# Chunked linear attention and a two-layer block: x of the first two chunks written in the order of q's columns, with a written-out order of operations

## Chip, cores and metric

The kernel runs on one core of a Trainium2 chip. The metric is the device time in microseconds (us) of one execution. The core has five engines with an instruction queue each: TensorE (PE), VectorE (DVE), ScalarE (ACT), GpSimd (POOL) and SyncE (SP). SP only issues DMAs here; ACT and POOL issue some too. Each engine works its queue strictly in order and waits on semaphores for the others.

## What is computed

q, k and v are float32 of shape (4, 8, 768, 64): batch, heads, tokens, head width. For each head, attention without softmax runs over blocks of 64 tokens with a decay lam:

```
intra = (q_b k_b^T * Dmask) v_b
inter = (q_b * lam_pow) kv_state
out_b = intra + inter
kv_state = lam^64 * kv_state + (k_b * rev_pow)^T v_b
```

The heads of a token, side by side, are x (3072 tokens by 512), and the rest is

```
h = x @ w_in                  # 512 -> 2048
g = h + sin(alpha*h)^2 / (alpha + 1e-9)
out = g @ w_out               # 2048 -> 512
```

## The kernel before

The 3072 tokens are worked on in six chunks of 512. The attention of a chunk is done by four *quads*; a quad is 256 tokens of four heads. Quads 0 to 3 (function quad0) make chunk 0, quads 4 to 7 chunk 1, and the sixteen behind them (function quad) make chunks 2 to 5 by another layout. In quad0, t = 4 ch + 2 u + jj: u is the half of the chunk's tokens, jj the half of the heads.

Every operation is recorded with a tag, and the documents name operations by these tags, with the quad or the chunk and block behind them:

- qs, ks, vs: scaling of q (L936) and k (L949) and the cast of v (L963, L966) to bf16
- Tq, Tk: transposes on TensorE (L977); cT: their copies to SBUF (L980)
- S: the product of q and k (L1020); mask: its masking on VectorE (L1025)
- Z: the product of k and v (L1037); Zi, Z with a digit, Zs: casts and sums of the state (L1056, L1110, L1122)
- I, O: what state and masked product give to the attention's output (L1067, L1082), in two PSUM banks
- x: the cast of these banks to xT in bf16 (L1099 for chunks 0 and 1, L1283 behind them)
- A: x @ w_in for one block of 128 of the 2048 columns (L1330); an ending h0 or h1 is a half of the chunk, and a final e the part of a product that is started early
- sin, sq, g: sine on ACT (L1342), its square on ACT (L1349), VectorE or POOL (L1350), and g on VectorE (L1354); g frees the PSUM bank of A
- B: g @ w_out (L1407); oh, o: its eviction (L1416, L1420, L1423); st: the store (L1426)
- w0 to w3 and w4 to w7: the loads of the blocks of w_in and w_out on POOL's queue (L793, L800, L805)
- quad k4.0 and the like: the loads of chunks 0 and 1 on SP's queue (L891, L897), load k4.0 and the like those of later chunks (L775, L784)

In chunks 0 and 1, q is loaded so that a partition holds four successive tokens. Its transposed columns therefore stand in the order (e, b): first the tokens 4b, then 4b+1, and so on, in groups of 32 within a block of 128. S, I and O carry this order on into the PSUM banks. piece_x puts the tokens back in order as it casts: it reads 32 elements in a row and writes every fourth element of xT:

```
o = xT[x][:, 2*jj:2*jj+2, 256*u:256*u+256].rearrange("p a (i b e) -> p i a e b", i=2, e=4)
i = M_ps[:, a:b + 1:b - a, :].rearrange("p i (a e b) -> p i a e b", e=4, b=32)[:, :, 0:2]
```

The order of the work is found at build time by a planner (Program.schedule). It plays through the program with a cost for each operation and takes, on each engine, the operation that can start first, with small hand-set shifts of rank (TURN), earliest times for the weight loads (HOLD) and an added lateness for loads (LATE). It hands out the six PSUM banks, fills long gaps of TensorE before 60 us with products of zeros (L754; one is counted at 0.4267 us until COLD, 0.2157 after it), and adds a wait of a POOL operation for the last VectorE operation that shares a port with it. GATE lets a load of chunk 1 wait for a named operation; a name that no operation bears is no wait, and q has no gate with a second digit of 1. In the plan a cast of x costs 0.585 us on ACT and 0.65 on VectorE. ENG0, ENG1, X0, X1, SQ0 and SQ1 say which engine does an operation; BOTH in X1 splits a cast in a half on ACT and one on VectorE.

From chunk 1's A on, TensorE alternates A of the next chunk with B of the current one, and one quad of a later chunk is worked in between.

Of the kernel before, what the change touches and what calls it, by code (L numbers as in the profile page):

```python
# [242 lines left out]
          'x7.1': -20},  # L243
    SQ0=('DVE', 'ACT', 'POOL', 'POOL', 'DVE', 'ACT', 'ACT', 'POOL', 'ACT', 'ACT', 'ACT', 'ACT', 'ACT', 'DVE', 'DVE',
         'POOL'),
# [11 lines left out]
    CUTS=(0, 256, 384, 512),  # L257
    GATE={'q4.0': 'Tk1', 'q6.0': 'Tk0', 'q6.1': 'A0.4', 'v4.0': 'O2'},
    SPLIT=(1, 1, 0, 1),
# [6 lines left out]
          {'c': ('ACT', 'DVE'), 'k': 'DVE', 'p': 2, 'q': 'DVE', 'v': 'ACT', 'w': 'DA', 'z': 'DD'},  # L266
          {'c': ('DVE', 'ACT'), 'k': ('DVE', 'POOL'), 'p': 2, 'q': 'DVE', 'v': 'ACT', 'w': 'AA', 'z': 'AD'},
          {'c': ('DVE', 'ACT'),
# [5 lines left out]
           'z': 'AA'}),  # L274
    X0=('ACT', 'DVE', 'DVE', 'DVE'),
    ENG1=({'c': 'ACT', 'k': ('POOL', 'DVE'), 'p': 0, 'q': 'DVE', 's': 0, 'v': 'POOL', 'w': 'DD', 'z': 'DD'},
          {'c': ('DVE', 'ACT'),
# [24 lines left out]
    LATE={'D': 0.5, 'l': 1, 'q': 0},  # L302
    COLD=10.5,
    FSL=0.05,
)

# [30 lines left out]
class Program:  # L337
# [9 lines left out]
    def __init__(self, nbanks, fill=None, fill_until=0.0, window=12, hold=None, turn=None):  # L347
        self.hold, self.turn = hold or {}, turn or {}
        self.ops = []
        self.writer = {}  # L350
        self.readers = {}
        self.slots = {}
        self.nbanks = nbanks
        self.fill = fill
        self.fill_until = fill_until
        self.window = window
        self.nb = 0
        self.late = {}

    def bank(self):  # L360
# [3 lines left out]
    def add(self, eng, fn, lat=0.0, occ=None, reads=(), writes=(), slot=None, work=0.0, weight=1.0, after=(),  # L364
# [3 lines left out]
        if port is None:  # L368
            port = "whole" if eng == "POOL" else ""
        self.ops.append(op)  # L370
# [37 lines left out]
    def schedule(self):  # L408
# [9 lines left out]
        left = {op: len(op.deps) + len(op.soft) for op in ops}  # L418
        ready = {op: self.hold.get(op.tag, 0.0) for op in ops}
        free = {e: 0.7 for e in self.ENGINES}  # L420
        pend = {e: [] for e in self.ENGINES}
# [8 lines left out]
        def held(e="SP"):  # L430
            return sum(q[0].desc * (q[1] / q[0].work if q[0].work else 1.0) for q in queues[e]) - self.RING
# [25 lines left out]
        while done < len(ops) or any(queues.values()):  # L457
            best = None
            for e in self.ENGINES:
                if e == "PE":  # L460
                    picks = []
                    for i, op in enumerate(pe[:60]):
# [16 lines left out]
                else:  # L479
                    if not pend[e] or (e == "SP" and held() > 0):  # L480
                        continue
                    can = pend[e] if e != "ACT" or held(e) <= 0 else [o for o in pend[e] if o.slot is None]
                    if not can:
                        continue
# [90 lines left out]
            order.append(op)  # L575
            done += 1
            for u in op.soft_users:
# [82 lines left out]
def bass_lightning_attn__then__act_snake_kernel(  # L660
# [12 lines left out]
    DM = H * D  # L673
# [23 lines left out]
    with es:  # L697
# [58 lines left out]

        P = Program(NPS, fill=zero_mms, fill_until=60.0, window=12, hold=HOLD, turn=TURN)
        P.narrow_until = TUNE["NARROW"]
        P.cold, P.slack = TUNE["COLD"], TUNE["FSL"]
        P.late = TUNE["LATE"]  # L760
        rec = P.add
# [108 lines left out]
        def alpha_ops():  # L870
            rec("ACT", lambda e: e.dma_start(alpha_r[:, :], moe_alpha.rearrange("(m p) -> m p", p=128)),
                writes=["alpha_r"], slot="alpha", work=0.1, weight=9.0, desc=16, tag="alpha")
            vb = P.bank()
# [28 lines left out]
        def quad0(ch, u, jj, engs, engs2):  # L902
# [187 lines left out]
            def piece_x(eng="ACT"):  # L1090
                def io(y):
                    o = xT[x][:, 2 * jj:2 * jj + 2, 256 * u:256 * u + 256].rearrange("p a (i b e) -> p i a e b", i=2, e=4)
                    a, b = banks[0].i, banks[1].i
                    i = M_ps[:, a:b + 1:b - a, :].rearrange("p i (a e b) -> p i a e b", e=4, b=32)[:, :, 0:2]
                    return (o, i) if y is None else (o[:, y], i[:, y])
# [298 lines left out]
        def grp_B(c, s4, m4):  # L1394
# [23 lines left out]
            if m4 == 3:  # L1418
# [147 lines left out]
```

## Time and profile before

| | us |
|---|---|
| three runs: median (lowest to highest) | 222.88 (221.7 to 223.21) |
| the profiled execution's own time | 222.66 |
| its span, first to last instruction | 220.9 |
| TensorE busy (of it zero products, L754) | 204.7 (8.7) |
| VectorE, ACT, POOL busy | 132.7, 132.1, 122.3 |
| mean granted clock | 0.992 of full |

The span is the time from the first to the last instruction; 1.76 us lie around it. Busy times are of engines, and overlap. In the slices of the page a digit is the busy share in tenths, and PEclk the clock that was granted to TensorE. The chain of waits goes back from the end of a window: at each step to what released it, so the lines in order of time are the work that nothing hid. A group's line gives the engine, the tile written and read, shape and count, then its total busy time, the mean in ns, and the idle time before it with what ended it. By the trace, x0 runs on ACT from 15.99, x1, x2 and x3 on VectorE from 21.43, 24.42 and 26.20, and x7 on ACT from 66.36.

### The profile page before, as it was taken

The page shows a single profiled execution, that of the slowest core. Times are in us where ns is not written, and L with a number is a line of the kernel's source. Part 1 is how long each engine was busy: PE and PEld are TensorE (multiplying, and loading weights), DVE is VectorE, ACT ScalarE, POOL GpSimd, SP SyncE. Part 2 cuts the span into 40 slices and gives each one's busy share as a digit, 9 for nine tenths or more (in the row PEclk, how much of TensorE's full clock was granted, in tenths as well). Part 3 has the DMA queues.
Part 4 walks back from the last instruction along what each step waited for, and adds up shares of the span by engine and source line. Part 5 has one row for each costly group of instructions (what it writes and reads, how often), then busy time and mean ns, then how long its engine had stood idle before and what let it go on. Part 6 is the DMA issues. An engine that isn't in the chain of part 4 may idle for free.

```text
span 220.9 us, 5170 instructions
## 1 busy us (share of the span) xinstructions
PE 204.7 (93%) x2109; PEld 108.8 (49%) x2140; DVE 132.7 (60%) x229; ACT 132.1 (60%) x245; POOL 122.3 (55%) x136
## 2 busy tenths in 40 slices
PE   7766798899998999999999999999999999999995
PEld 6344563544566455444455445554454444444445
DVE  5668959947997877364584477665446335544300
ACT  3634289933569975687567767866564545544211
POOL 3692084315034964099999599987455554354000
PEclk9999699999999999999999999999999999999999
DMA  6999999999579999999998989962011011100123
GB/s 202 306 259 223 221 284 205 218 185 194 136 179 204 163 196 163 252 198 175 188 233 175 238 180 191 219 147 72 3 47 50 0 47 47 50 32 16 66 76 99
DMA packets 86490, 33.91 MB, mean 154 GB/s; under 512 B 68274, under 2 KB 83522, under 8 KB 86466
## 3 DMA queue, kind: packets, MB, share of 16 engines
q1 hardware_dynamic: 77552, 22.88, 56.1%
q0 software_dynamic: 4752, 4.19, 11.7%
q10 hardware_dynamic: 4162, 6.50, 8.6%
q8 instruction: 17, 0.28, 0.5%
q14 instruction: 7, 0.06, 0.1%
HBM read 27.27 MB, written 6.29 MB: 152 GB/s over the span
## 4 chain that ended last, share of the span: by engine, by line
PE 76%; ACT 9%; DVE 8%; issue 3%; POOL 2%; ACTq 0%; DVEq 0%
PE M_ps L1330 33%; PE M_ps L1407 31%; ACT t L1342 3%; PE M_ps L1231 2%; DVE gT L1354 2%; DVE S_m L1025 2%; PE M_ps L1375 2%; ACT v L1166 2%; PE M_ps L754 1%; PE M_ps L1211 1%; PE A_ps L1191 1%; PE M_ps L977 1%; DVE xT L1099 1%; PE A_ps L1020 1%; ACT xT L1099 1%
## 5 line engine op out<-in xcount | busy, mean ns | idle before, releaser
L1354 DVE SCALAR_TENSOR_TENSOR gT<-u,r_sb,M_ps 128x512 bf16<-128x512 bf16 (+1 forms) x108 | 72.1, 685 | 52.1 <-POOL u L1350 50.1
L1350 POOL TENSOR_TENSOR u<-t 128x512 bf16<-128x512 bf16 x70 | 71.9, 1041 | 51.6 <-ACT t L1342 44.7
L1330 PE MATMUL M_ps<-xT,w 128*128 128x512 bf16 (+1 forms) x426 | 92.3, 358 | 3.1 <-DVE xT L1099 1.1
L1342 ACT ACTIVATE t<-M_ps,alpha_sb 128x512 bf16<-128x512 f32 (+1 forms) x108 | 67.1, 641 | 36.6 <-PE M_ps L1330 36.0
L1407 PE MATMUL M_ps<-w,gT 128*128 128x512 bf16 x347 | 86.1, 379 | 2.8 <-issue 1.9
L1330 PEld LDWEIGHTS M_ps<-xT,w 128*128 128x128 bf16 x432 | 41.4, 98 | 44.5 <-issue 4.1
L1407 PEld LDWEIGHTS M_ps<-w,gT 128*128 128x128 bf16 x368 | 34.2, 98 | 39.5 <-DVE gT L1354 1.2
L1155 POOL TENSOR_TENSOR qk<-k,Lk 128x512 bf16<-128x512 f32 x16 | 16.7, 1044 | 8.4 <-DVE Zq L1122 8.4
L1203 DVE TENSOR_TENSOR S_m<-A_ps,maskl 128x768 bf16<-128x768 f32 x16 | 15.3, 956 | 8.6 <-PE A_ps L1191 8.4
L1423 ACT COPY osb<-M_ps 128x512 f32<-128x512 f32 x20 | 11.7, 586 | 12.0 <-PE M_ps L1407 11.9
L1155 POOL TENSOR_TENSOR qk<-q,Lq 128x512 bf16<-128x512 f32 x16 | 16.6, 1041 | 1.9 <-DVE u L1350 1.9
L1306 ACT CAST Zq<-Zf 64x256 bf16<-64x256 f32 x24 | 9.7, 402 | 6.2 <-DVE Zf L1300 4.6
L1283 ACT CAST xT<-M_ps 128x512 bf16<-128x512 f32 x16 | 9.4, 585 | 5.5 <-PE A_ps L1191 5.4
L1025 DVE TENSOR_TENSOR S_m<-A_ps,maskq 128x1024 bf16<-128x1024 f32 x8 | 9.8, 1221 | 2.1 <-PE A_ps L1020 1.9
L754 PE MATMUL M_ps<-zeros 128*128 128x128 bf16 (+1 forms) x45 | 8.7, 350 | 1.4 <-DVE zeros L813 1.2
L949 POOL TENSOR_TENSOR qk<-k,Lk 128x256 bf16<-128x256 f32 (+1 forms) x7 | 4.7, 682 | 9.3 <-DVE qk L949 9.3
L1166 ACT CAST v<-v 128x512 bf16<-128x512 f32 x16 | 9.6, 620 | 0.1
L1349 ACT ACTIVATE u<-t 128x512 bf16<-128x512 bf16 x14 | 8.8, 642 | 0.2
L805 POOL DMA_DIRECT2D w<-in_moe_w_out_dram x4 | 3.1, 784 | 8.7 <-DVE Zf L1110 8.7
L1099 ACT CAST xT<-M_ps 128x256 bf16<-128x256 f32 (+1 forms) x5 | 4.8, 963 | 4.9 <-PE M_ps L1037 2.6
L1383 DVE COPY osl<-M_ps 128x128 f32<-128x128 f32 x1 | 0.3, 291 | 10.9 <-PE M_ps L1375 10.9
L1099 DVE CAST xT<-M_ps 128x512 bf16<-128x512 f32 (+1 forms) x6 | 6.1, 1010 | 0.9 <-PE M_ps L1037 0.5
(87 smaller groups left out, 150.5 us busy)
## 6 DMA issues: line engine op xcount, KB each, us to landing
out_dram<-osb ACTq DMA_DIRECT2D x23, 256.0 KB, 2.2
q<-in_q_dram SPq DMA_DIRECT2D x20, 256.0 KB, 4.8
k<-in_k_dram SPq DMA_DIRECT2D x34, 128.0 KB, 4.4
v<-in_v_dram SPq DMA_DIRECT2D x32, 128.0 KB, 4.7
v<-in_v_dram SPq DMA_DIRECT2D x8, 256.0 KB, 8.6
w<-in_moe_w_out_dram POOLq DMA_DIRECT2D x4, 512.0 KB, 10.4
k<-in_k_dram SPq DMA_DIRECT2D x6, 256.0 KB, 9.4
w<-in_moe_w_in_dram POOLq DMA_DIRECT2D x3, 512.0 KB, 12.8
```

The lines of the kernel that those rows point to most:

```text
L754: last = e.matmul(m_ps[i][:, 0:c], zeros[:, 0:128], zeros[:, 0:c])
L1025: rec("DVE", lambda e: e.tensor_tensor(S_m[jm][:, :, :].rearrange("p (h a b) c -> p h a (b c)", h=2, a=2), Av().rearrange("p h (a x) -> p ...
L1099: en, lambda e, y=y, en=en: (e.copy if en == "ACT" else e.tensor_copy)(*io(y)),
L1155: rec(en, lambda e, L=L, gs=slice(g0, g0 + m): e.tensor_tensor(o[:, :, gs], i[:, :, gs], L, ALU.mult), *(((0.65, 0.58) if en == "DVE" else ...
L1166: rec("ACT", lambda e: e.copy(o, i), 0.613, 0.51, reads=rd, writes=[f"v2.{c}"], tag=f"vs{t}")
L1203: rec("DVE", lambda e: e.tensor_tensor(S_m[jm][:, :, :].rearrange("p (a b) c -> p a (b c)", a=4)[:, :, 0:192], A_ps[:, :, :].rearrange("p ...
L1330: last = e.matmul(m_ps[vb.i][:, N * i:N * i + N], w1[:, kc, 128 * mm:128 * (mm + 1)], xT[x][:, kc, ts], start=(kc == 0 and i == 0), stop=( ...
L1342: rec("ACT", lambda e, i=i, mm=mm: e.activation(t16[tt][:, N * i:N * i + N], m_ps[vb.i][:, N * i:N * i + N], ACTF.Sin, scale=alpha_sb[:, m ...
L1350: return e.tensor_tensor(u16[tt][:, :], t16[tt][:, :], t16[tt][:, :], ALU.mult)
L1354: rec("DVE", lambda e, i=i, mm=mm: e.scalar_tensor_tensor(out=gT[g][:, mm, ts], in0=u16[tt][:, N * i:N * i + N], scalar=r_sb[:, mm:mm + 1] ...
L1407: last = e.matmul(m_ps[vb.i], gT[g][:, m, 128 * s4:128 * (s4 + 1)], w2[:, m, :], start=(m == 0 or (split and m == 8)), stop=(m == NM - 1 o ...
L1423: rec("ACT", lambda e: e.copy(osb[o][:, :], m_ps[vb.i]), 0.585, 0.48, reads=[vb.key], writes=[f"o.{o}"], frees=[vb], tag=f"o{gsi}")
```

## The change

Four things, in one diff.

1. piece_x writes xT in the order of the banks, in runs of 128, so the columns of xT in chunks 0 and 1 stand in the order (e, b). A and B work column by column and keep that order. The store of an output tile of these chunks sends partition p = 32 e + b to row 4 b + e. The planner's costs stay as they were.
2. Some engines: sq0.2h0 goes from POOL to VectorE, Zs2.0 and Zs2.1 from ACT to VectorE, x3 from VectorE to ACT, Zs4.0 and Zs4.1 from VectorE to ACT.
3. The gates: q4.0 and q6.0 have none now, k6.0 waits for mask3, v6.1 for Tk3; v4.0 keeps O2. COLD goes from 10.5 to 11.5.
4. Program.schedule gets an ORDER: for each engine a list of all tags, and it takes the next of the list and nothing else. With it HOLD and LATE are off; banks, zero products and added waits still come from the plan. Against the order of before (the tags that moved):

- PE: Tq3 behind Tk0 and no longer before Tk2; A0.14 before A0.6, A0.10h1 before A0.10h0; Tk6 behind I5; O5 before Z6; I6 before S7. From A1.2h0 on nothing changes.
- DVE: memsets and mask copies at the start; x3 left out, Zs2.1, sq0.2h0 and Zs2.0 behind Zs3.0; g0.5h1 before g0.4h1, ks6.1 before sq0.14, vs7 behind g0.11h0, Zs4 left out, g1.4h0 before g1.1h0.
- ACT: x3 behind sin0.5h0, Zs2 left out; Zs4.0 before x5.0, and Zs4.1 behind it, both after Zi6 and st2.
- POOL: the iota for E_i3 (c6) behind the masks; ks4.0 before w2; sq0.2h0 left out; ks5.0 before vs4; ks9 before qs9.
- SP: load k4.1 before quad k6.1, and two pairs of loads of chunks 5 and 6 turned round.

```
-    SQ0=('DVE', 'ACT', 'POOL', 'POOL', 'DVE', ...
+    SQ0=('DVE', 'ACT', 'DVE', 'POOL', 'DVE', ...
-    GATE={'q4.0': 'Tk1', 'q6.0': 'Tk0', 'q6.1': 'A0.4', 'v4.0': 'O2'},
+    GATE={'k6.0': 'mask3', 'q4.1': 'mask0', 'q6.1': 'A0.2', 'v4.0': 'O2', 'v6.0': 'A0.2', 'v6.1': 'Tk3'},
...
-          {'c': ('DVE', 'ACT'), 'k': ('DVE', 'POOL'), 'p': 2, 'q': 'DVE', 'v': 'ACT', 'w': 'AA', 'z': 'AD'},
+          {'c': ('DVE', 'ACT'), 'k': ('DVE', 'POOL'), 'p': 2, 'q': 'DVE', 'v': 'ACT', 'w': 'DD', 'z': 'AD'},
...
-    X0=('ACT', 'DVE', 'DVE', 'DVE'),
-    ENG1=({'c': 'ACT', 'k': ('POOL', 'DVE'), 'p': 0, 'q': 'DVE', 's': 0, 'v': 'POOL', 'w': 'DD', 'z': 'DD'},
+    X0=('ACT', 'DVE', 'DVE', 'ACT'),
+    ENG1=({'c': 'ACT', 'k': ('POOL', 'DVE'), 'p': 0, 'q': 'DVE', 's': 0, 'v': 'POOL', 'w': 'AA', 'z': 'DD'},
...
-    COLD=10.5,
+    COLD=11.5,
+    ORDER={'ACT': [..., 'x0', 'cT3.1', 'Zs0.0', 'Zi3.1', 'vs1', 'Zi3.0', 'Zs1.1',
+                   'sin0.4h0', 'sin0.5h0', 'x3', 'Zs3.1', 'sin0.2h0', 'sin0.3h0', ...
+           'DVE': ['c1', 'c2', 'c7', 'c20', 'c9', 'c23', 'c10', 'c24', 'c19', 'c25', 'c26', 'c27', 'c22', 'c12',
+                   'c15', 'qs1', 'qs3', 'ks2.0', 'cT3.0', 'c31', 'cT0.1', 'qs2', ...
+                   'mask3', 'Z1.1', 'x2', 'sq0.4h0', 'Z3.1', 'g0.4h0', 'g0.5h0', 'Z2.1', 'Zs3.0',
+                   'Zs2.1', 'sq0.2h0', 'Zs2.0', 'g0.2h0', ...
+           'PE': ['ln lam', 'Tq1', 'alpha T', 'Tk2', 'Tk0', 'Tq3', 'Tq0', 'Tq2', 'S0', ...
+           'POOL': ['c5', 'c4', 'c3', 'c18', 'c8', 'c21', 'c28', 'c6', 'ks2.1', 'ks0', 'c30', 'w1', 'qs0', 'w0',
+                    'vs0', 'ks3.0', 'w0b', 'w3', 'ks4.0', 'w2', 'qs5', 'w4', 'w5', 'w6', 'sq0.7', ...
...
+        given = {e: [named[x] for x in self.given.get(e, ()) if x in named and named[x].eng == e] for e in self.ENGINES}
...
+                    if head[e] is not None:
+                        can = [head[e]] if head[e] in can else []
...
-        P = Program(NPS, fill=zero_mms, fill_until=60.0, window=12, hold=HOLD, turn=TURN)
+        P = Program(NPS, fill=zero_mms, fill_until=60.0, window=12, hold=HOLD if not TUNE["ORDER"] else {}, turn=TURN)
...
-        P.late = TUNE["LATE"]
+        P.late = TUNE["LATE"] if not TUNE["ORDER"] else {}
+        P.given = TUNE["ORDER"]
...
-                    o = xT[x][:, 2 * jj:2 * jj + 2, 256 * u:256 * u + 256].rearrange("p a (i b e) -> p i a e b", i=2, e=4)
+                    o = xT[x][:, 2 * jj:2 * jj + 2, 256 * u:256 * u + 256].rearrange("p a (i y) -> p i a y", i=2)
...
-                    i = M_ps[:, a:b + 1:b - a, :].rearrange("p i (a e b) -> p i a e b", e=4, b=32)[:, :, 0:2]
+                    i = M_ps[:, a:b + 1:b - a, :].rearrange("p i (a y) -> p i a y", y=128)[:, :, 0:2]
...
-                rec("ACT", lambda e: e.dma_start(out[row0:row0 + 128, :], osb[o][:, :]),
+                rows = out[row0:row0 + 128, :]
+                if c < 2:
+                    rows = bass.AP(out.tensor, row0 * DM, [[DM, 4], [4 * DM, 32], [1, DM]])
+                rec("ACT", lambda e: e.dma_start(rows, osb[o][:, :]),
```

More of the change, by code (lines that the diff above doesn't have):

```diff
@@ L243 @@
           'x7.1': -20},
-    SQ0=('DVE', 'ACT', 'POOL', 'POOL', 'DVE', 'ACT', 'ACT', 'POOL', 'ACT', 'ACT', 'ACT', 'ACT', 'ACT', 'DVE', 'DVE',
+    SQ0=('DVE', 'ACT', 'DVE', 'POOL', 'DVE', 'ACT', 'ACT', 'POOL', 'ACT', 'ACT', 'ACT', 'ACT', 'ACT', 'DVE', 'DVE',
          'POOL'),
@@ L302 @@
     LATE={'D': 0.5, 'l': 1, 'q': 0},
-    COLD=10.5,
+    COLD=11.5,
     FSL=0.05,
+    ORDER={'ACT': ['lam', 'c0', 'quad k0.1', 'alpha in', 'c11', 'c13', 'c14', 'c16', 'c17', 'c29', 'alpha', 'cT1.0',
[100 rows of a table added]
 )
@@ L358, in __init__ @@
         self.late = {}
+        self.given = {}
+        self.plain = 0
     def bank(self):
@@ L369, in add @@
             port = "whole" if eng == "POOL" else ""
+        if not tag:
+            tag = f"c{self.plain}"
+            self.plain += 1
         self.ops.append(op)
@@ L419, in schedule @@
         ready = {op: self.hold.get(op.tag, 0.0) for op in ops}
+        named = {op.tag: op for op in ops}
+        given = {e: [named[x] for x in self.given.get(e, ()) if x in named and named[x].eng == e] for e in self.ENGINES}
+        given = {e: iter(L + [None]) for e, L in given.items()}
+        head = {e: next(L) for e, L in given.items()}
         free = {e: 0.7 for e in self.ENGINES}
@@ L461, in schedule @@
                     picks = []
-                    for i, op in enumerate(pe[:60]):
+                    for i, op in enumerate(pe[:60] if head[e] is None else (head[e],)):
                         if i >= self.window and picks:
@@ L576, in schedule @@
             done += 1
+            if op is head[e]:
+                head[e] = next(given[e])
             for u in op.soft_users:
@@ L871, in alpha_ops @@
             rec("ACT", lambda e: e.dma_start(alpha_r[:, :], moe_alpha.rearrange("(m p) -> m p", p=128)),
-                writes=["alpha_r"], slot="alpha", work=0.1, weight=9.0, desc=16, tag="alpha")
+                writes=["alpha_r"], slot="alpha", work=0.1, weight=9.0, desc=16, tag="alpha in")
             vb = P.bank()
```

98 rows, old and new, of the table ORDER are left out of this document.

## The prediction

> **What bounds the kernel now.** I read the page's busy shares and slices first, then the busy time by stage, the chain of waits up to 70 us, the granted clock in half microseconds, and the groups by line and shape. Operations go by their tags (x1 is the cast that writes x of quad 1, A the first product, B the second).
>
> ```profile
> PE 204.7 (93%) x2109; PEld 108.8 (49%) x2140; DVE 132.7 (60%) x229; ACT 132.1 (60%) x245; POOL 122.3 (55%) x136
> PE   7766798899998999999999999999999999999995
> PEclk9999699999999999999999999999999999999999
> ```
>
> TensorE is the bound from slice 13 on. Its gaps lie in front, where chunks 0 and 1 are prepared, and slice 5 (22 to 28 us) has a lower clock. The stages; after each length stand the busy times of TensorE, its weight loads, VectorE, ACT and POOL, then the granted clock, the DMA share and GB/s:
>
> ```profile
> 1.18:22.88 21.70, 15.89 (x259) 10.37 (x263) 15.66 (x37) 10.02 (x22) 11.64 (x18) 0.99 1.14 260
> 22.88:27.64 4.76, 4.09 (x43) 2.78 (x45) 4.27 (x7) 1.09 (x3) 0.00 (x0) 0.67 1.20 222
> 27.64:36.74 9.10, 8.31 (x47) 4.46 (x49) 6.56 (x16) 8.13 (x17) 7.11 (x8) 1.00 1.19 252
> 36.74:45.34 8.60, 7.67 (x48) 4.16 (x50) 8.14 (x16) 8.40 (x18) 2.52 (x4) 1.00 1.21 209
> 67.83:80.00 12.17, 12.06 (x81) 6.70 (x84) 10.09 (x21) 11.84 (x25) 9.56 (x10) 1.00 1.11 192
> ```
>
> From 67.83 TensorE is full, so a microsecond won before it is a microsecond at the end. From 27.64 ACT is 89% full and from 36.74 98%, VectorE 72 and 95%, so an earlier start there counts only if they start earlier too. The chain of waits up to 70 us:
>
> ```profile
> 20.29 1.23 DVE S_m L1025
> 21.52 1.22 DVE xT L1099
> 22.74 0.14 issue
> 22.88 1.44 PE M_ps L1330 x6
> ...
> 26.20 1.30 DVE xT L1099
> 27.50 0.14 issue
> 27.64 1.05 PE M_ps L1330 x8
> ...
> 65.02 1.47 ACT t L1342 x4
> 66.49 1.20 ACT xT L1099
> 67.69 0.14 issue
> 67.83 1.91 PE M_ps L1330 x16
> ```
>
> TensorE waits in turn for x1, x3 and x7. What such a cast costs, and what one with whole rows costs:
>
> ```profile
> L1099 DVE CAST xT<-M_ps 128x512 bf16<-128x512 f32 x3 | 3.9, 1291 | 0.5 <-PE M_ps L1037 0.5
> L1099 ACT CAST xT<-M_ps 128x512 bf16<-128x512 f32 x2 | 2.6, 1308 | 1.6 <-PE M_ps L1037 1.6
> L1283 ACT CAST xT<-M_ps 128x512 bf16<-128x512 f32 x16 | 9.4, 585 | 5.5 <-PE A_ps L1191 5.4
> L1383 ACT COPY osl<-M_ps 128x256 f32<-128x256 f32 x1 | 0.4, 373 | 1.1 <-PE M_ps L1375 1.1
> ```
>
> L1283 is the same cast for later chunks: two banks in, the same pieces of 128, written in order. The old L1099 writes every fourth element.
>
> **The change, part by part.** The sum is made against the profiled execution: 222.66 us, of which 220.9 is span and 1.76 lies around it; the median shown, 222.88, is 0.22 above.
>
> *The casts.* On ACT a whole one goes from 1.31 to 0.585 (row L1283), a half from 0.73 to 0.37 (row L1383). VectorE has no such cast; its add over 512 columns from PSUM (L1420) takes 0.68 and its copy of 128 (L1383) 0.29, so I take 0.68 for a whole and 0.42 for a half. The Trainium skill (SBUF — State Buffer, Door 1: The DMA port swizzle) has lines of 16 bytes at full bandwidth from two hits a line; every fourth bf16 hits each line twice, so by it nothing is saved here and the sum would be 0.5. The rows speak against it.
>
> *x1* (VectorE, right behind mask2): 1.29 to 0.68, and TensorE stands still for it. Gain 0.6; it was followed by A0.4h0e, whose weights (block w1, issued at 9.23, landed 8.4 later) are there at 17.6. x0 on ACT is 0.7 shorter, but the next operation there (cT3.1) waits for TensorE's Tk3 until 17.55: nothing, unless Tk3 comes earlier.
>
> *x3 moves to ACT*, behind sin0.4h0 and sin0.5h0. Before, x2 and x3 followed each other on VectorE and x3 ended 4.6 us after A0.4h0e began. Now, counted from that same start: the two sines end at 3.51 (26.39), O3 at 3.3, so x3 ends at 3.51 + 0.59 = 4.1. Gain 0.5. If a bank or the sines hold it, 0; if TensorE is at full clock there (below), 1.1.
>
> *The order on ACT, VectorE and POOL, 28 to 45 us.* Zs2.0 and Zs2.1 leave ACT (two of about 0.2 of engine time); ACT works without a break from 28.71 to 45.2, so 0.4. sq0.2h0 goes from POOL, where it stood behind w4 to w6 (28.04 to 30.34), to VectorE's idle 2.4 us from 29.04: the bank it holds is free some 2.4 us earlier (g0.2h0 began at 31.44). TensorE's wait for a bank there is 0.63 at 36.1. I take 0.3; bounds 0 and 1.0 (the wait and ACT's 0.4).
>
> *The front.* The E_f copy now waits for the last iota, behind POOL's masks: from 1.53 to some 2.5. VectorE has 1.28 idle before lnL at 4.80, which hides it; without that cover it costs up to 0.2. Tq3 moves behind Tk0 and its copy behind 9.3 us; q2o of quad 2 then starts at about 10.2 instead of 9.65, but it ended at 10.94 anyway, as POOL's w1 and qs0 work at that time: nothing. No planned lateness is added to loads any more, so fewer zero products stand before ln lam (27 run until 4.24, while lnlam is done at 2.9): 0 to 0.5 gained. I take 0 for all of this, bounds -0.2 and 0.5.
>
> *POOL's ks4.0 before w2.* It ran from 16.06 and VectorE's ks3.1 beside it took 0.93, where a sibling takes 0.42. One weight DMA (0.76) earlier it meets ks1 instead. ks3.1 leads to Tk3 and on to mask2. I take 0.2; bounds -0.3 (ks1 is hit instead) and 0.5. w2 goes out about 0.8 later; it landed at 31.5 and A0.8 reads it after 36: hidden.
>
> *SP's gates.* q4.0 no longer waits for Tk1 (SP stood from 12.86 to 16.31); 512 KB enter the queue 3.4 us earlier, but v6.1 behind it now waits for Tk3 (17.5), about when it went out before (17.66). v4.0's wait for O2 stays, k6.0's for mask3 (24.3) is over when SP gets there at 28 or 29. All of chunk 0 was issued before 8.6: 0. Without holds w4 to w6 go out behind qs5 (19.4) and not at 28.04; POOL's queue still had w2 in flight until 31.5, so they wait there, not others: 0, bounds -0.3 and 0.2.
>
> *x4 to x7, Zs4 to ACT.* TensorE's gap before 67.83 is 0.60 and the chain behind it is x6.0, two v casts, four sines, x7, all on ACT: 0.36 and 0.73 shorter. The gap goes; then TensorE is late itself. Gain 0.6, bounds 0 and 0.6. VectorE loses Zs4 (0.45) before x5.1, and S7 now stands behind I6 (0.44) where mask7 waited for VectorE's o1 anyway. Other gaps from 40 to 62 us (0.48 for cT6.0, 0.36 for g, 0.45 for Zi4) keep their order; I take 0.2 for them, bounds -0.3 and 0.5.
>
> *Stores.* Eight of them write 2 KB rows four rows apart; before, the same 128 rows in sequence. They take 0.34 on ACT's queue and land in 2.2 to 5.6; the tile is used again six tiles later: 0.
>
> Sum: 0.6 + 0.5 + 0.3 + 0 + 0.2 + 0 + 0.6 + 0.2 = 2.4. 222.66 - 2.4 = 220.3 us, 1.2% below the median.
>
> **The rivals.** *The start is earlier, but ACT and VectorE give it back* (221.5): x1's 0.6 and x7's 0.6 are sure to be seen at TensorE, the other 1.2 lies in stretches where ACT or VectorE is nearly full and a fixed order lets a late operation block its whole engine. For it: 8.40 of 8.60 us of ACT from 36.74. Against: ACT itself starts its sines earlier. 222.66 - 1.2 = 221.5.
>
> *TensorE keeps its clock* (219.2): in before it runs at half clock from 22.6 to 26.0:
>
> ```profile
> 22.50:23.00 0.50, 0.12 (x1) 0.14 (x2) 0.50 (x3) 0.24 (x1) 0.00 (x0) 0.60 1.27 222
> 25.50:26.00 0.50, 0.50 (x24) 0.50 (x16) 0.20 (x1) 0.47 (x2) 0.00 (x0) 0.50 1.22 216
> ```
>
> Six pieces of A took 1.44 there. With full clock O3 and the sines come earlier and x3 with them; 1.1 in place of 0.5 and up to 0.5 at A0.1: 220.3 - 1.1 = 219.2. For it: TensorE waits 0.8 us less before. Against: its start is as thin as it was.
>
> *Slower: more of the work at half clock* (225.4). The planner now counts a zero product as slow (0.4267) until 11.5 and not 10.5 us, so the six before Tq0 (1.46 us of 2.57) become about three, and the lateness that made others is gone. One spell at half clock lasted 3.4 us; where TensorE is 91% busy, as from 27.64, it costs 1.7. Two more would eat up the gain (223.7), three give 225.4. The Trainium skill (TensorE: Matmul & The Clock Gate, Part 1: The HAM clock gate) has the clock halved after an idle window of about 3.4 us, with windows that run free of the kernel. By that rule the thinner front is a risk; the length in this trace agrees, 3.4 us.
>
> *The casts stay as long* (222.2): if it is not the order of the write that makes L1099 long, x1 and x7 gain nothing and x3, behind the sines, ends at 3.51 + 1.31 = 4.8 and not 4.6: 0.2 - 0.2 + 0.3 + 0.2 = 0.5. This is what the skill's rule on lines would give. Against it stands row L1283.
>
> **How the numbers follow.** Forecast 0.46 (219.8 to 220.9), full clock 0.14, given back 0.26, casts as long 0.04, slower 0.10. A measurement of this kernel can tell about 1% from no change: below 220.65 is faster, above 225.1 slower. Faster: three quarters of the forecast (0.35), all of full clock, a sixth of given back (0.04): 0.53. Slower: 0.10, where two or three half-clock spells come together. Same: 0.37. The range reaches from below full clock with the bounds of the front (218.6) to the casts as long (222.6); outside lie slower and under 0.1 at the lower end.
>
> **What would show it.** Casts L1099: ACT 0.59, VectorE near 0.68, halves under 0.45. A's first product near 22.1, its second wait over near 26.4, no wait of TensorE for xT over 0.3 near 67. If the gap at 36.1 grows or new ones stand between 40 and 62 us, the gain was given back. The granted clock by half microseconds from 9 to 40 us tells the clock's part. I am wrong if the first A starts at 22.1 and the span is still over 220.2, or if TensorE waits for a weight block or a load, which I put at nothing.

## The result and the profile after

The changed kernel takes 240.0 us (median of 4, 238.16 to 241.34), the kernel before on the same chip 222.56 (221.7 to 223.21). The ratio is 1.078, with a 95% interval of 1.069 to 1.087. The forecast was 220.3; its range ended at 222.6. The profiled execution took 241.34 us, its span 239.4. Here and below, ratios and their intervals leave out single executions more than 1.5% above the fastest of the same kernel; medians do not.

TensorE's busy time, its slices and its clock, and what the DMAs moved, from the page of the changed kernel:

```profile
PE 214.2 (89%) x2135; PEld 108.6 (45%) x2135; DVE 129.8 (54%) x229; ACT 131.8 (55%) x246; POOL 121.3 (51%) x135
PE   8797986899869998974975899999999999999995
PEclk9999999999997999996799799999999999999999
GB/s 202 286 236 227 259 218 211 151 204 171 102 128 169 198 159 178 110 149 181 158 172 154 119 252 189 186 224 113 67 3 44 47 44 29 15 47 44 44 88 92
```

A slice is 6.0 us here. The first five are as full as before or fuller. Holes stand in slices 7 and 12 and again in 18, 19, 21 and 22 (102 to 132 us). In these last TensorE was full before. The lower clocks stand in or next to such holes. GB/s falls to 102 in slice 11 (60 to 66 us), just before the second hole. The stretches of the prediction, cut at the same times, in the same columns:

```profile
1.18:22.88 21.70, 18.24 (x269) 10.93 (x269) 15.70 (x39) 9.55 (x22) 9.71 (x17) 1.00 1.11 251
22.88:27.64 4.76, 4.36 (x52) 2.86 (x50) 3.91 (x13) 3.33 (x8) 3.15 (x5) 1.00 1.21 237
36.74:45.34 8.60, 5.82 (x34) 2.57 (x33) 5.82 (x12) 6.92 (x15) 3.30 (x3) 1.00 0.85 177
67.83:80.00 12.17, 10.10 (x61) 4.79 (x59) 7.01 (x14) 7.82 (x15) 6.97 (x8) 0.86 1.19 165
```

There are two losses. The small one lies at 36.74 to 45.34: TensorE works 5.82 us and not 7.67, and the lead won in front is gone. The large one begins after 56 us, where the stores of the first two chunks begin: a stretch that had 12.06 of 12.17 us of work has 10.10, at 0.86 of the clock.

The casts came out as forecast, and the front started earlier than forecast. The casts of x, by shape:

```profile
L1214 ACT CAST xT<-M_ps 128x512 bf16<-128x512 f32 x3 | 1.8, 586 | 1.6 <-PE M_ps L1152 1.6
L1214 DVE CAST xT<-M_ps 128x512 bf16<-128x512 f32 x2 | 1.4, 675 | 0.0
L1214 DVE CAST xT<-M_ps 128x256 bf16<-128x256 f32 x3 | 1.3, 422 | 0.5 <-PE M_ps L1197 0.5
L1214 ACT CAST xT<-M_ps 128x256 bf16<-128x256 f32 x3 | 1.1, 372 | 2.4 <-PE M_ps L1197 1.7 <-PE M_ps L1152 0.7
```

Whole casts cost 586 and 675 ns, halves 372 and 422; the prediction had 585, 680, 370 and 420. By the single records of the trace the first A begins at 21.72 (22.88 before, 22.1 by the forecast), the A that needs x2 at 24.30 (26.31 before), and the A that needs x3 at 24.96 (27.64 before, 26.4 by the forecast). All of it runs at full clock, where the profile of before has half clock from 22.6 to 26.0. The chain of waits shows how this lead of 2.7 us goes:

```profile
18.29 21.82 DMA q<-in_q_dram
40.10 0.07 issue
40.17 1.56 POOL q2o L1051
41.73 0.14 issue
41.87 0.40 PE M_ps L1092 x4
...
42.72 1.57 DVE gT L1469 x4
44.29 0.05 issue
44.34 3.63 PE M_ps L1522 x16
```

q4.0 (512 KB) is under way for 21.8 us, counted from the start of its issue; that issue begins 2 us later than before (18.29 for 16.31) and takes SP 6.87 us in place of 1.30. qs6 on POOL waits for q4.0, Tq6 for qs6, and from 44.34 TensorE is where it was before at 44.46.

The large loss shows on SP, which issues the loads. Its issues and transposes behind the first four stores, in the changed kernel (start, length, then the operation):

```profile
58.59 6.90 SPq L1293 DMA_TRANSPOSE qkT<-qk  x2
65.53 2.71 SPq L890 DMA_DIRECT2D q<-in_q_dram  x1
68.28 3.66 SPq L899 DMA_DIRECT2D v<-in_v_dram  x1
71.98 1.51 SPq L890 DMA_DIRECT2D q<-in_q_dram  x1
73.54 2.37 SPq L899 DMA_DIRECT2D k<-in_k_dram  x1
75.95 0.64 SPq L899 DMA_DIRECT2D v<-in_v_dram  x1
```

and in the kernel before:

```profile
62.06 3.38 SPq L1178 DMA_TRANSPOSE qkT<-qk  x2
65.49 0.62 SPq L775 DMA_DIRECT2D q<-in_q_dram  x1
66.16 0.65 SPq L784 DMA_DIRECT2D v<-in_v_dram  x1
66.84 0.62 SPq L775 DMA_DIRECT2D q<-in_q_dram  x1
67.50 0.69 SPq L784 DMA_DIRECT2D v<-in_v_dram  x1
```

Issues of 0.62 to 0.69 us become issues of 1.5 to 3.7 until 75.9. (Slow ones occur before too: two loads took 3.42 us together from 70.53.) The stores' own issues on ACT are longer as well (before, all 23 took 0.34 to 0.36). Runs 5 and 6 will show that the 0.55 among them goes with the form of the pattern, and not with the loads:

```profile
56.16 0.66 ACTq L1544 DMA_DIRECT2D out_dram<-osb  x1
58.34 0.55 ACTq L1544 DMA_DIRECT2D out_dram<-osb  x1
58.98 1.30 ACTq L1544 DMA_DIRECT2D out_dram<-osb  x1
61.95 0.55 ACTq L1544 DMA_DIRECT2D out_dram<-osb  x1
```

In that time the DMA engines are busier and move less. After, then before, the same two stretches (the last two columns are DMA share and GB/s):

```profile
60.00:65.00 5.00, 4.33 (x80) 3.06 (x78) 3.86 (x10) 3.83 (x11) 0.00 (x0) 1.00 0.85 99
65.00:70.00 5.00, 5.00 (x62) 3.85 (x60) 3.56 (x11) 4.93 (x13) 2.29 (x3) 1.00 1.35 128
```

```profile
60.00:65.00 5.00, 4.91 (x81) 3.27 (x79) 4.90 (x11) 3.29 (x9) 2.04 (x2) 1.00 0.65 170
65.00:70.00 5.00, 4.27 (x57) 3.27 (x57) 3.54 (x12) 4.97 (x13) 0.94 (x1) 1.00 1.06 226
```

By the packet records of the trace, the 256-byte packets of the loads took 87 ns on average from 60 to 65 us and 103 from 65 to 70; in the kernel before it is 18 to 31 ns in every such 5-us slice. From 65 to 73 us only 160 to 200 of them start in a microsecond; in the kernel before it is 390 to 920.

The late loads reach TensorE, which also waits for qkT, a transpose that a DMA on SP's queue does. The waits of TensorE between 56 and 145 us, the three longest of the changed kernel, then the longest one of before that has a releaser:

```profile
PE M_ps L1445 <- DVE gT L1469: 4.1, 1, 4.1
PE M_ps L1326 <- DMA qkT<-qk: 3.7, 1, 3.7
PE A_ps L1306 <- DMA qkT<-qk: 2.1, 1, 2.1
```

```profile
PE M_ps L1330 <- ACT xT L1099: 0.6, 1, 0.6
```

In the changed kernel POOL and ACT stand for loads of k and v (us in total, times; before, no operation is listed as waiting for these loads):

```profile
  POOL qk L1270: 11.7, 4
  ACT v L1281: 10.3, 3
```

Last, the page's line for the queue of the stores, after and then before (packets, MB, share):

```profile
q10 hardware_dynamic: 4066, 6.50, 8.1%
```

```profile
q10 hardware_dynamic: 4162, 6.50, 8.6%
```

The bytes are the same and the 2 KB packets too; 96 of the small completion packets are missing. The eight changed stores have 12 fewer each. If each DMA engine that serves a store ends its share with one such packet, these stores ran on 4 engines and the others on 16. The outermost size of the new store is 4.

From this came theory A: the store's outermost size of 4 confines it to four DMA engines. Each then gets 64 KB of every 256, which is 32 packets of 2 KB. The packet records bear the four out: the 2 KB packets of the first four changed stores are in flight 3.2 to 3.7 at a time (their summed time over the length of the store), those of the first store before 13.4. One after the other without a gap, these four stores fill the time from 58.2 to 73.1 us, and in the microsecond that starts at 73 the 256-byte packets are back at 28 ns. By the theory, a load that is spread over all engines ends only when these four get to its share, and SP's queue fills behind it. The rivals: the scattered rows are slow to write; or the loss comes from the order, the gates and the engine moves, whose late q4.0 is the first thing that goes wrong.

### The profile page after: what moved, and what is told of

Its sections match the earlier page's. It is cut to its first block, busy times and chain, and to the rows that moved or that the text cites. A ratio compares the mean times of both kernels' runs of the same rounds, so it can differ in the third digit from the quotient of the medians.

```text
span 239.4 us, 5188 instructions
## 1 busy us (share of the span) xinstructions
PE 214.2 (89%) x2135; PEld 108.6 (45%) x2135; DVE 129.8 (54%) x229; ACT 131.8 (55%) x246; POOL 121.3 (51%) x135
## 3 DMA queue, kind: packets, MB, share of 16 engines
q1 hardware_dynamic: 77552, 22.88, 57.3%
q10 hardware_dynamic: 4066, 6.50, 8.1%
## 4 chain that ended last, share of the span: by engine, by line
PE 51%; DMA 20%; SPq 14%; POOL 6%; issue 3%; ACT 3%; DVE 1%; ACTq 0%; POOLq 0%
PE M_ps L1522 25%; PE M_ps L1445 19%; DMA q<-in_q_dram 9%; SPq L1012 6%; POOL u L1465 4%; DMA k<-in_k_dram 4%; SPq L899 4%; DMA qkT<-qk 4%; DMA v<-in_v_dram 3%; SPq L890 2%; POOL qk L1270 2%; PE M_ps L1490 1%; SPq L1006 1%; PE M_ps L1346 1%; SPq L1293 1%
## 5 line engine op out<-in xcount | busy, mean ns | idle before, releaser
L1445 PE MATMUL M_ps<-xT,w 128*128 128x512 bf16 (+1 forms) x432 | 95.1, 364 | 5.5 <-DVE gT L1469 4.9
L1465 POOL TENSOR_TENSOR u<-t 128x512 bf16<-128x512 bf16 x69 | 70.7, 1040 | 55.4 <-ACT t L1457 55.4
L1522 PE MATMUL M_ps<-w,gT 128*128 128x512 bf16 x368 | 92.7, 387 | 1.0 <-DVE gT L1469 0.8
L1318 DVE TENSOR_TENSOR S_m<-A_ps,maskl 128x768 bf16<-128x768 f32 x16 | 15.3, 956 | 20.9 <-PE A_ps L1306 20.8
L1281 ACT CAST v<-v 128x512 bf16<-128x512 f32 x16 | 9.6, 617 | 10.4 <-DMA v<-in_v_dram 10.3
L868 PE MATMUL M_ps<-zeros 128*128 128x512 bf16 (+1 forms) x44 | 11.1, 388 | 1.2 <-DVE zeros L928 1.2
L1326 PE MATMUL M_ps<-qkT,Zq 128*128 128x128 bf16 x56 | 5.4, 218 | 5.1 <-DMA qkT<-qk 3.7
L1326 PEld LDWEIGHTS M_ps<-qkT,Zq 128*128 128x128 bf16 x56 | 4.0, 97 | 9.3 <-issue 5.4
L1051 POOL TENSOR_TENSOR q2o<-q,Lq 128x512 bf16<-128x512 f32 x3 | 3.7, 1219 | 8.0 <-DMA q<-in_q_dram 8.0
L1306 PE MATMUL A_ps<-qkT 64*64 64x128 bf16 (+1 forms) x256 | 5.8, 210 | 2.1 <-DMA qkT<-qk 2.1
```

What stands on the lines that cost most here:

```text
L868: last = e.matmul(m_ps[i][:, 0:c], zeros[:, 0:128], zeros[:, 0:c])
L1318: rec("DVE", lambda e: e.tensor_tensor(S_m[jm][:, :, :].rearrange("p (a b) c -> p a (b c)", a=4)[:, :, 0:192], A_ps[:, :, :].rearrange("p ...
L1445: last = e.matmul(m_ps[vb.i][:, N * i:N * i + N], w1[:, kc, 128 * mm:128 * (mm + 1)], xT[x][:, kc, ts], start=(kc == 0 and i == 0), stop=( ...
L1465: return e.tensor_tensor(u16[tt][:, :], t16[tt][:, :], t16[tt][:, :], ALU.mult)
L1522: last = e.matmul(m_ps[vb.i], gT[g][:, m, 128 * s4:128 * (s4 + 1)], w2[:, m, :], start=(m == 0 or (split and m == 8)), stop=(m == NM - 1 o ...
```

## The experiments

All ratios are to the kernel before, run beside it on the same chip.

**1. The store of before, all else changed.**

```
-                if c < 2:
-                    rows = bass.AP(out.tensor, row0 * DM, [[DM, 4], [4 * DM, 32], [1, DM]])
```

> The changed kernel with the old store (128 rows in sequence) for all chunks; the output's rows of the first two chunks stand in the order of q's columns. Theory A, the eight stores whose outermost dimension is 4 hold up all loads behind them: about 15 to 17 us go away, 221 to 225 us, and no 256-byte packets of 90 ns and more between 55 and 70 us. Theory B, the order and the gates make the loads late from the start (k4.0 and q4.0 landed at 21.8 and 40.1) and the lateness grows: 236 to 240 us.

Measured: 219.05 us, ratio 0.980 (0.975 to 0.984), faster than theory A's range. q10 has 4162 packets again, and the 256-byte packets take 22 to 27 ns from 55 to 70 us.

**2. The kernel before with the new store alone.**

> The kernel before with nothing but the new store for the first two chunks; the output's rows there stand in another order. Theory A: 13 to 18 us slower than before, 236 to 241 us, with the loss behind the first store at 57 us. Theory B: within 1% of before.

Measured: 239.4 us, ratio 1.075 (1.067 to 1.083), 4066 packets. With run 1 it settles where the loss lies: the store costs all of it, and the rest of the change taken together is a gain.

**3. Each store cut in four of 32 rows.** The rows come out in the right order, and each store has an outermost size of 32.

```
+                    for y in range(4):
+                        rows = bass.AP(out.tensor, (row0 + y) * DM, [[4 * DM, 32], [1, DM]])
+                        rec("ACT", lambda e, y=y, rows=rows: e.dma_start(rows, osb[o][32 * y:32 * y + 32, :]), ...
```

> The changed kernel with each of the eight stores cut into four of 32 rows, so that the outermost dimension is 32 and no longer 4; rows as the reference has them. Theory A: as the plain store, plus three more issues of 0.35 us on ACT for each of eight tiles, mostly beside TensorE's work: 221 to 226 us. Theory A in another form, it is the step between the rows in memory and not the outermost 4: 235 to 241 us. Theory B: 236 to 241 us.

Measured: 231.52 us, ratio 1.038 (1.031 to 1.045): half of the loss remains, and the expectation is missed. The 256-byte packets take 38 ns from 60 to 65 us and 18 to 31 in the other slices, so the loads are nearly free. By the trace the cost has moved to ACT: its issues of stores make up 13% of the chain of waits from 56 to 140 us, some 11 us. No run tests this on its own. Some of the issues, three or four at a time:

```profile
62.62 1.44 ACTq L1548 DMA_DIRECT2D out_dram<-osb  x3
65.73 2.47 ACTq L1548 DMA_DIRECT2D out_dram<-osb  x4
96.13 3.01 ACTq L1548 DMA_DIRECT2D out_dram<-osb  x4
```

Four issues at 0.34 would be 1.36 us a store and 1.0 more than one; here they take 1.8 to 3.0 us, and casts and sines wait behind them.

**4. The kernel before with the new casts alone** (the output rows of the first two chunks then stand in the order of q's columns).

> The kernel before with nothing but the new order of x (the casts write runs of 128) and the old stores; the output's rows of the first two chunks stand in the order of q's columns. The forecast's terms for x1 and x7 (0.6 each) and a part of x3 without its move (0.6): 220.5 to 222 us. If the start of chunk 0 is given back by loads that come late, as the trace of the changed kernel shows up to 45 us: 222 to 223.5 us.

Measured: 221.02 us, ratio 0.988 (0.983 to 0.993). The casts alone gain 1.2%.

**5. Outermost size or scattered rows.** Three stores in the kernel before, told apart by their pattern alone:

```
e6:  bass.AP(out.tensor, (c*S + 32*s4)*DM, [[128*DM, 4], [DM, 32], [1, DM]])
e7:  bass.AP(out.tensor, row0*DM,          [[DM, 32], [32*DM, 4], [1, DM]])
e8:  bass.AP(out.tensor, row0*DM,          [[DM, 8], [8*DM, 16], [1, DM]])
```

> The kernel before with only the stores of chunks 0 and 1 changed: each sends its 128 partitions as four groups of 32, a group to 32 rows in sequence, the groups 128 rows apart; the outermost size is 4 as in the change, the rows of a group are neighbours. The output rows of the first two chunks stand in another order. Theory A1 (the outermost size 4 confines the store to four DMA engines): q10 has 4066 packets, and the time is near that of the changed store alone, 236 to 241 us. Rival A2 (what is slow is that 2 KB rows next to each other are written four rows apart, to scattered addresses): 4162 packets or not, 222 to 225 us.

> The kernel before with only the stores of chunks 0 and 1 changed: partition p goes to row 32 (p mod 4) + p div 4, so neighbours are 32 rows apart, and the outermost size is 32. The output rows of the first two chunks stand in another order. Theory A1 (outermost size, thus the number of DMA engines, decides): 16 engines, q10 with 4162 packets, 222 to 225 us, no different from before. Rival A2 (scattered rows are slow): 230 to 241 us.

> The kernel before with only the stores of chunks 0 and 1 changed: outermost size 8 with neighbours in a group 8 rows apart. The output rows of the first two chunks stand in another order. A test of the dose. Theory A1: eight DMA engines serve a store (64 completion packets fewer on q10 than in before, 4098), each gets twice and not four times its share; if the loss goes with the extra load of the engines that serve it (3 units for four engines, 1 for eight, over the 16.2 us that four cost), about 5 us: 225 to 231. Rival (a store on fewer than 16 engines costs its fixed price, whatever the number): 236 to 241. Rival (scattered rows): 230 to 241 with 4162 packets.

| store | outermost size | neighbours apart | q10 packets | us | ratio (95%) |
|---|---|---|---|---|---|
| of the change (run 2) | 4 | 4 rows | 4066 | 239.4 | 1.075 (1.067 to 1.083) |
| e6 | 4 | 1 row | 4066 | 240.72 | 1.077 (1.071 to 1.084) |
| e8 | 8 | 8 rows | 4098 | 227.96 | 1.020 (1.014 to 1.027) |
| e7 | 32 | 32 rows | 4162 | 223.19 | 1.001 (0.998 to 1.004) |

The lines of e8 and of e7:

```profile
q10 hardware_dynamic: 4098, 6.50, 9.1%
```

```profile
q10 hardware_dynamic: 4162, 6.50, 8.2%
```

Rows next to each other do not help (e6), rows 32 apart do no harm (e7). The time goes with the packets that are missing, 12, 8 and 0 a store. Eight engines cost 5.3 us and four 16 and 18, near the 1 to 3 of the extra load on each engine. The 256-byte packets follow: 94 and 142 ns in e6 from 60 to 65 and from 65 to 70 us, 30 and 34 in e8 (before 25 and 21). The longer issue on ACT does not follow: it is 0.55 us in e6 and in e7 and 0.61 in e8 (the first store 0.65 to 0.73), so it comes with the three-level pattern and costs nothing that can be seen in e7. The Trainium skill (DMA: Bandwidth & Descriptors, Why a DMA increments its semaphore by 16 and not by 1) says that a transfer runs on the largest number of engines up to 16 that divides the outermost sizes of both its patterns, which gives 4, 8 and 16 here. The packet counts agree with it in each run. The prediction did not weigh this rule.

**6. Where the same store meets no loads.** Eight later stores, of chunks 3 and 4, get the form of the change in the kernel before; by then the loads are over, and the stores lie 7 to 8 us apart.

```
+                if c in (3, 4):
+                    rows = bass.AP(out.tensor, row0 * DM, [[DM, 4], [4 * DM, 32], [1, DM]])
```

> The kernel before with only the stores of chunks 3 and 4 (eight of 256 KB, from about 160 to 205 us) in the form of the change: outermost size 4, rows four apart, so the rows within each block of 128 of these chunks stand in another order. By the profile of before the loads are over at about 150 us. Theory A (what costs is that the loads of q, k and v wait on the DMA engines that a store fills): nothing is left to hold up, 222 to 224 us, 0.995 to 1.005 of before, with 4066 packets on q10. Rival E (the store itself costs: it takes so long that ACT's queue or the output tiles stand): the same eight stores cost 8 to 18 us, 230 to 241.

Measured: 221.82 us, ratio 0.997 (0.994 to 1.000). The store ran on as few engines, by the page of this run:

```profile
q10 hardware_dynamic: 4066, 6.50, 10.0%
```

and TensorE was as busy beside it as before (this run's stretch, then that of before):

```profile
155.00:205.00 50.00, 49.42 (x326) 23.41 (x330) 24.01 (x34) 25.52 (x40) 24.91 (x24) 1.00 0.14 37
```

```profile
155.00:205.00 50.00, 49.42 (x325) 23.45 (x329) 23.79 (x35) 25.99 (x42) 24.92 (x24) 1.00 0.09 32
```

The packet records show the four engines by themselves here: the packets of such a store are in flight 3.7 at a time and take 4.3 us all in all, those of a store of before at the same place 13.3 at a time and 0.83 us. The store is five times as long, its issue on ACT takes 0.55 us without any loads, and nothing waits for it. At this spacing rival E is out. It doesn't carry the loss among the loads either: in the changed kernel no operation is listed as waiting for a store, and the issues of the eight stores on ACT sum to 5.3 us (2.8 before), while ACT alone waits 10.3 us for loads of v. What the store costs is the loads that share its engines.

**7. The order put right at q's transposes.** Tq of chunks 0 and 1 becomes four products with the unit matrix into fp32 PSUM, written to every fourth column; S, x and the output then stand in the order of the tokens, and the store is the old one.

```
...
+                            d = m_ps[tb.i].rearrange("p (c y) -> p y c", y=4)
+                            for y in range(4):
+                                last = e.matmul(d[:, y, :], src(y), ident[:, :])
...
```

> The changed kernel, with the order of the tokens put right at q's transposes and not at the store: Tq of chunks 0 and 1 multiplies each of the four pieces by the unit matrix and writes its 32-column groups to every fourth fp32 column of the bank, so the copy cT, the masks, x and the output all stand in the order of the tokens, and the store is the old one (128 rows in sequence). All computed values are those of the reference. If only the eight stores made the changed kernel slow (theory A), this one is as fast as the one with the old store, 219.05 us, plus what the eight copies cT of q cost now that they read 512 fp32 columns and not 512 bf16 (0.68 for 0.42 us on VectorE by the rows, of which two lie on the way to x0 and x1): 218.8 to 220.5, 1.2 to 2% faster than before. Rival: TensorE, with four products for four transposes and a longer copy, starts S0 later, and the front gives back 1 us or more: 220.5 to 222.5.

Measured: 220.77 us, ratio 0.988 (0.981 to 0.994); a second time (below) 0.992 (0.987 to 0.997). It computes all of the reference and is far faster than the changed kernel. Against the kernel before its gain is about 1% by these ratios and not certain: the median of all executions is 220.77 beside 222.65 the first time, and 222.64 beside 222.5 the second. What the traces show of its price against run 1 lies on two engines. On VectorE it is the copy of q:

```profile
L1099 DVE CAST qTo<-M_ps 128x512 bf16<-128x512 f32 x5 | 3.5, 692 | 7.0 <-PE M_ps L1093 6.9
```

The copy of 512 bf16 columns took 425 ns in run 1. On TensorE the 32 products take 327 ns each, 5.1 us in all, where the 32 transposes of q took 220 ns each and 2.9 us. The measured time lies just above the range of the one theory and in that of the rival; the interval reaches into both.

**8. The terms of the sum.** The order, gates and engine moves without the new casts and store:

> The changed kernel with the casts of x of before (every fourth element) and its store: what is left are the engine moves, the gates and the written-out order. The casts alone gained 2.2 us (1.2%), and casts and rest together 4.2 (2.0%). Theory B (the gains add up, as the prediction's sum has it): the rest alone gains about 2, thus 0.8 to 1.0%. Rival (x3's move to ACT and the start of the long A pay only with the short cast, which the prediction has as casts as long, a gain of 0.5 us): 0 to 0.4% faster.

Measured: 221.39 us, ratio 0.994 (0.991 to 0.997): 0.6%, between the two expectations, so this does not tell whether the gains add up exactly. Beside it, on the same chip, run 1 again, then run 1 with w2 ahead of ks4.0, and run 1 with the gates of before:

> The changed kernel with the plain store of before once more, as the measure for the next two on the same chip; the rows of the output's first two chunks stand in the order of q's columns. 0.975 to 0.985 of before, as the first time (0.980).

> The changed kernel with the plain store of before (rows of the first two chunks in the order of q's columns) and, on POOL, w2 ahead of ks4.0 as before the change. The prediction gave ks4.0 ahead of w2 a gain of 0.2 us (bounds -0.3 and 0.5), with ks4.0 taken to run about 0.8 us after its old place; in the profile of the changed kernel ks4.0 stands 7 to 9 us for its load, and w2 goes out 7 us late. If the prediction's term is right, w2 first is 0.2 us slower than the plain store alone. Rival C (POOL's stall costs the end something): w2 goes out at about 15, w4 to w6 and the qs and ks behind them earlier, and it is 0.5 to 1.5 us faster. If all of it is hidden behind ACT and VectorE: within 0.5 us.

> The changed kernel with the plain store of before (rows of the first two chunks in the order of q's columns) and the gates of before: q4.0 waits for Tk1, q6.0 for Tk0, v6.1 and k6.0 for nothing. The prediction put the gates at 0 (bounds -0.3 and 0.2 us). If that is right: within 0.5 us of the plain store alone. Rival D (with the new gates the loads of chunks 1 and 2 crowd those of chunk 1 that are due first, and k4.0 and q4.0 are late for that): k4.0 lands earlier, POOL's wait for it is under 4 us, and the time is 0.5 to 1.5 us shorter.

Measured: 221.36 us, 0.987 (0.980 to 0.993); 219.23 us, 0.983 (0.978 to 0.988); 220.17 us, 0.984 (0.979 to 0.989). The repeat of run 1 lies just above the ratio that was expected of it. The three can't be told apart. The last two runs put the gates to the test once more, on the version of run 7:

> The version with the order put right at q's transposes and the gates of before (q4.0 waits for Tk1, q6.0 for Tk0, v6.1 and k6.0 for nothing). If the gates cost nothing, as the prediction has it: 0.981 to 0.994 of before, like the same version with the new gates. Rival D (with the new gates q4.0 lands at 40 us in some executions, as in the profile of the changed kernel, and the executions lie apart for that): the median falls to 0.978 to 0.985 and the highest of the executions lies under 221.5 us.

> The version with the order put right at q's transposes and all else of the change, once more, as the measure for the one with the old gates on the same chip: 0.981 to 0.994 of before (0.988 the first time). By rival D its executions spread from 219 to 223 us and those with the old gates do not.

Measured: 221.04 us, 0.993 (0.989 to 0.998) with the old gates; 222.64 us, 0.992 (0.987 to 0.997) with the new. Old gates spread from 219.65 to 222.75, new ones from 219.48 to 223.76: rival D is not borne out. What the profiles do show is that q4.0 comes late in some executions, with either set of gates. In the eight profiles of versions with the new order and the old store, POOL waits between 10 and 50 us for q's loads, all in all, 3.8 to 5.4 us where the span is 216.5 to 218.4 (runs e1, e5, e9, e12), and 6.3 to 8.1 us where it is 219.5 to 221.0 (e10, e11, e14, e15). The eight differ in more than this wait, so that it makes the span longer is not shown, and why the same load lands sooner in one execution than in another was not found.

## Why the prediction was wrong, point by point

**Stores: 0.** This is the step that failed. The prediction had "They take 0.34 on ACT's queue and land in 2.2 to 5.6; the tile is used again six tiles later: 0". It priced the issue and the landing of the store, taken from rows of the old store, as if only the next writer of its tile could wait for it. It did not ask which DMA engines would serve the new pattern, nor what else was queued on them. Run 2 puts this step at 16 to 17 us, runs e6 to e8 lay it to the outermost size, run e13 to the loads. That the issue takes 0.34 was wrong too: it takes 0.55 to 0.66, once 1.30. The prediction named its own test, TensorE waiting for a load, "which I put at nothing": that is what came, through SP's late issues.

**Casts, x1 and x7.** Right in mechanism and in the price of one, 586 and 675 ns. TensorE's wait of 0.6 us for x7 is gone in runs 1 and 4 and stands at 0.5 in run e9, whose casts are the old ones. In sum the casts alone gain 1.2% in run 4 (0.7 to 1.7), thus 1.6 to 3.9 us. The forecast gave x1 and x7 together 1.2 us, and the expectation of run 4 added 0.6 for x3; that this is too low is not shown. The rival in which the casts stay as long is out. The rule on lines that this rival rested on does not hold here: every fourth bf16 took 1282 to 1295 ns in run e9 on either engine, about twice as long as in runs of 128. (The old cast also goes in runs of 32 elements and not of 128; no run tells that apart from the step of four.)

**x3's move.** The forecast had 0.5 us for it with the short cast and a loss of 0.2 with the long one. The A that needs x3 begins at 27.64 in the profile of before, but at 26.95 and 27.12 in runs e7 and e13, whose front is the same and at full clock. With the rest alone and long casts it begins at 26.05 (e9), with the casts alone at 25.41 (run 4), with both at 24.88 (run 1). These are single profiles. By them the rest, with the move in it, gains some 1 us at this place with the long cast too, where the forecast expected the move to lose.

**The rest.** For the version with the old casts and the old store the prediction's own sum is that of its rival with long casts, 0.5 us or 0.2%. Run e9 gains 0.6% (0.3 to 0.9): these terms came out larger, as the start behind x3 has it. Casts and rest together gain 2.0% in run 1 and 1.3% in its repeat, where the sum was 1.1%. So without the failed step the time would have fallen into the range, 219.05 and 221.36 us on either side of 220.3. That it would have been met is in part luck, since the start behind x3, the clock and the loads of the front came out otherwise than written.

**ks4.0 before w2, 0.2, and SP's gates and POOL's w4 to w6, 0.** These went another way than written, at little price. ks4.0 did not simply run earlier: POOL stands for the load of k4.0 (the wait in the changed kernel, then that for q):

```profile
POOL qk L1064 <- DMA k<-in_k_dram: 10.0, 2, 7.3
POOL q2o L1051 <- DMA q<-in_q_dram: 8.0, 2, 6.4
```

w2 goes out at 22.56 and not at 15.3 or 0.8 later. Nor did q4.0 enter the queue 3.4 us earlier, as the prediction has it: its issue begins 2 us later than before. Runs e11, e12 and e14 find no price that can be measured for either step, though the late q4.0 goes with a longer span in the eight profiles above.

**The clock.** The condition of the rival in which TensorE keeps its clock did come true, and the prediction gave it 0.14: from 22.6 to 26.0 us the granted clock is 1.00 in the changed kernel and 0.50 in the profile of before. But the change need not have brought it. Runs e7 and e13 leave this front as it was, and their clock there is 1.00 too; of all 17 profiles only that of before and that of run 3 (0.62) are lower. The half-clock spell that the prediction read from one execution is not a fixed part of the kernel. Nor did full clock alone bring the 1.1 us by which that rival moved x3: the start behind x3 lies only 0.5 to 0.7 earlier in e7 and e13. The rival in which more runs at half clock did not take place as written. The half-clock spell of the changed kernel (0.71 of the clock from 70 to 75 us) stands behind a gap of TensorE of 2 us, at a time when loads are late, and the front, where fewer zero products were feared, is at full clock. The chance of 0.10 for slower was on another mechanism.

**Given back.** By 44 us the lead is lost in the changed kernel, as this rival has it, but to loads and not to full engines: from 36.74 to 45.34 ACT works 6.92 of 8.60 us, 8.40 before.

## What to carry to other kernels

Before a DMA's pattern is changed, read the outermost size of both sides: 4 and 8 cost 8% and 2% here, 32 nothing, even with neighbouring rows 32 apart. Price a store not by its issue and its own landing but by what queues on the engines that serve it: among the loads a store on four engines held up everything, and 100 us later the same store was free. And if data is to be put back in order, then of the ways tried here it was cheapest where a pass over the data exists anyway (a transpose, 0.11 us longer a piece on TensorE, its copy 0.27 us longer on VectorE), and dearer by a DMA with an outermost size of 4 or by four DMAs for one. Last, a stretch at half clock in one profile need not belong to the kernel: look at a second execution before a term is built on it.

## What was not expected of the hardware

- A store on four DMA engines slows loads that run on all of them: their 256-byte packets go from 18 to 31 ns to 81 to 142 ns on average between 60 and 70 us (changed kernel, e2, e6), and SP's issues of loads from about 0.65 us to between 1.5 and 3.7. Alone, such a store takes 4.3 us in place of 0.83 (e13).
- An issue of 256 KB on ACT takes 0.34 us with 128 rows in sequence and 0.55 to 0.73 with a three-level pattern, whether it runs on 4, 8 or 16 engines and whether loads are near or not; one in the changed kernel took 1.30. Four issues of 64 KB took 1.8 to 3.0 us beside loads, where four times 0.34 would be 1.4.
- A cast from PSUM that writes every fourth bf16, 32 in a run, takes 1.29 us for 128x512 on either engine, in runs of 128 it takes 0.59 on ACT and 0.68 on VectorE.
